# Attention in steps of two sequences, and a written order for TensorE in the middle blocks, in a fused retention, gated MLP and soft-MoE kernel

## The chip, the cores and the metric

One Trainium2 chip, one core. The metric is the device time of the whole kernel in microseconds (us). TensorE is called PE here, its weight loads PEld; VectorE is DVE, ScalarE ACT, GpSimd POOL, SyncE SP. SP's queue and ACT's queue issue the DMAs.

## What is computed

Three stages in a row, in float32, on 8 sequences of 576 tokens with 8 heads of 64 (4608 tokens, model width 512):

```python
scores = q @ k.T / sqrt(64);  ret = scores * gamma[h] ** (i - j)   # lower triangle only
x = heads_side_by_side(ret @ v)                                    # 4608 x 512
h = x @ w_in;  g = h * sigmoid(1.702 * h);  x = g @ w_out          # 512 -> 2048 -> 512
logits = x @ phi                                                   # 32 slots
d = softmax(logits, over tokens);  slot_input = d.T @ x            # 32 x 512
slot_out = 8 experts, 4 slots each: relu(slot_input @ w1) @ w2     # 512 -> 1024 -> 512
out = softmax(logits, over slots) @ slot_out                       # 4608 x 512
```

## The kernel before, in words

The 4608 tokens are cut into 12 blocks of 384 (`NB`), and a block's first MLP layer into 16 groups `fc` of 128 columns. `main_fc(n, fc)` (line 312) runs 12 matmuls into the PSUM tile `hp`: four 128-row pieces of x, each as high x high, high x low, low x high part (fp32r operands, full 128x128 weights, 384 columns). ACT writes the gated result to `gT`. `turn_fc` (324) turns each `gT` on DVE in 32x32 pieces, and after eight of them 16 DMAs on SP's queue finish the transposition into `nat` (line 349).

The second layer is never run over the tokens. w_out is folded with phi into `Wp` at the start, so `logits_group` (352) makes the expert scores `Lg` straight from `gT`, four matmuls a group on 32 weight columns each. `softmax_part(n)` (360) adds up the four parts with a matmul (`lt`), takes the running maximum, exponentiates to `dT`, and transposes it on PE (`dp`); `slots_part(n)` (400) accumulates `dn` times `nat` into `Sg`.

Attention makes x for the block after the one that the MLP is in. It goes in chunks of 64 tokens of one sequence, four head pairs. `chunk_out` (210) computes `Op`, eight matmuls of 128x64 weights; DVE scales it to `xs`, ACT rounds that to the high part of x and POOL subtracts to get the low part. `products` (175) adds the chunk's keys times values to the state `St` and multiplies keys and queries of the next chunk to `Sp`, both with 64x64 weights; DVE writes `St` and `Sp`, scaled by decay tables, back into the chunk's `pack` (lines 202, 203, 207, 208), from where the next `chunk_out` reads them. A chunk's q, k and v arrive by two DMAs of 256 KB, one on SP's queue and one on ACT's (`load_chunk`, 164); four packs rotate.

PE executes four weight shapes: 128x128 (`hp`, `lt`, and PE transposes of full size such as `tpw` and `tpg`), 128x64 (`Op`), 64x64 (`St`, `Sp`) and 128x32 (`Lg`, `Sg`); `dp` has a fifth, 64x128. A list `START` (50) orders the work of block 0, where the weights are loaded and split too. From block 1 on, the loop at line 489 emits the calls, chunks after the `fc` numbers in `CHUNK_AT` (55), and a scheduler with its own model of time puts the instructions of each engine in order. Block 11 has no attention beside it. In block 10 and after it the expert weights are prefetched (`prefetch`, 430), then come the experts and the output.

Of the kernel before, what the change touches and what calls it, by code (L numbers as in the profile page):

```python
# [38 lines left out]
NW2 = 9  # L39
# [15 lines left out]
CHUNK_AT = (0, 2, 5, 8, 10, 12)  # L55

# [55 lines left out]
def tile_kernel(ctx, tc, qkv, w_in, w_out, phi, w1, w2, consts, out):  # L112
# [44 lines left out]
    packs = []  # L157
    for i in range(NPACK):
        packs.append(pa.tile([128, 6, NP, C], F32, name=f"pack{i}", bufs=1))
    kts = [pa.tile([128, NP, D], F32, name=f"kt{i}", bufs=1) for i in range(2)]  # L160
# [3 lines left out]
    def load_chunk(g):  # L164
        t = packs[g % NPACK].rearrange("p c a d -> p (c a d)")
# [7 lines left out]
    halves = (slice(0, C), slice(C, 128))  # L173

    def products(g):

        n = g + 1
        more = g >= 0 and g % NPB < NPB - 1
        if more:
            if g % NPB == 0:  # L180
                St[g // NPB] = ps.tile([128, NP, D], F32, tag="St", name="St")
            s_, kk, t = St[g // NPB], kts[g % 2], packs[g % NPACK]
        if n < NT // C:
            u = packs[n % NPACK]
# [24 lines left out]

    def chunk_out(g):  # L210
        n, off = divmod(g * C, NB)
        t = packs[g % NPACK]
        Op = ps.tile([128, NP, C], F32, tag="r", name="Op", bufs=3)
        for p in range(NP):
            pe.matmul(Op[0:C, p, :], t[:, V0, p], t[:, Q0, p], start=True, stop=True)  # L215
            pe.matmul(Op[C:128, p, :], t[:, V1, p], t[:, Q1, p], start=True, stop=True)  # L216
# [3 lines left out]
        cols_ = slice(off, off + C)  # L220
        xs = pa.tile([128, NP, C], F32, tag="xs", name="xs")
        dve.tensor_tensor(xs, Op, osc, op=ALU.mult)  # L222
        act.copy(xh[n][:, :, cols_], xs)  # L223
        pool.tensor_tensor(xl[n][:, :, cols_], xs, xh[n][:, :, cols_], op=ALU.subtract)  # L224

    def chunk(g):

        if g + NPACK - 1 < NT // C:
            load_chunk(g + NPACK - 1)
        chunk_out(g)  # L230
        products(g)

    def chunk_items(n):

        if n >= NBLK:
            return []
        return [(CHUNK_AT[i], lambda g=g: chunk(g)) for i, g in enumerate(range(n * NB // C, (n + 1) * NB // C))]

# [70 lines left out]
    gT, pre, nat, Lg, dn = {}, {}, {}, {}, {}  # L309
    st = {"m": None, "corr": None}  # L310

    def main_fc(n, fc):
        g, fl = divmod(fc, GF)
        if fl == 0:
            gT[n, g] = pg.tile([128, GF, NB], F32, tag="gT", name="gT", bufs=2)
        hp = ps.tile([128, NB], F32, tag="h", name="hp", bufs=3)
        i = 0
        for dc in range(NDC):
            for a, b in ((0, xh), (0, xl), (1, xh)):
                pe.matmul(hp, wt[fc][:, a, dc, :], b[n][:, dc, :], start=(i == 0), stop=(i == 3 * NDC - 1))  # L320
                i += 1
        act.activation(gT[n, g][:, fl, :], hp, AF.Gelu_apprx_sigmoid)  # L322

    def turn_fc(n, fc):
# [19 lines left out]
        if fh == HF - 1:  # L344
            if hf == 0:
                nat[n] = pm.tile([128, NT128, 4, NFC, 32], F32, tag="nat", name="nat")
            for a in range(4):
                for b in range(4):
                    sp.dma_start(nat[n][32 * b:32 * b + 32, :, a, hf * HF:(hf + 1) * HF, :],
                                 pre[n, hf][32 * a:32 * a + 32, b])  # L350
# [8 lines left out]
    def softmax_part(n):  # L359
        Lp = pm.tile([128, 2, NB], F32R, tag="Lp", name="Lp")  # L360
# [28 lines left out]
        dp = ps.tile([128, NT128, 2 * NS], F32, tag="L", name="dp")  # L389
        for c in range(NT128):  # L390
            pe.transpose(dp[:, c, :], dT[0:2 * NS, c * 128:(c + 1) * 128], ident[0:2 * NS, 0:2 * NS])  # L391
# [5 lines left out]
                          mx.unsqueeze(2).to_broadcast([128, NT128, NS]), op=ALU.subtract)  # L397

# [25 lines left out]
    todo = [(0, i) for i in range(NFC // 2)] + first[9:] + second[:5] + first[:9] + second[5:]  # L424
# [31 lines left out]
    items = [lambda: products(-1)] + [lambda g=g: chunk(g) for g in range(2 * NB // C)]  # L456

    def step(x):
# [9 lines left out]
        elif x[0] == "A":  # L468
            items.pop(0)()
        elif x == "M":  # L470
            fc = st.setdefault("fc", 0)
            st["fc"] += 1
            main_fc(0, fc)
            turn_fc(0, fc)
            if fc % 4 == 1 and fc >= 5:
                logits_group(0, (fc - 5) // 4)
        elif x[0] == "T":
            load_chunk(int(x[1:]))
        else:
            raise ValueError(x)  # L480
# [6 lines left out]
    pw2 = None  # L487

    for n in range(1, NBLK):
        items = chunk_items(n + 1)  # L490
        ni, done = len(items), 0
        for fc in range(NFC):
            main_fc(n, fc)
            if n < LAST:
                turn_fc(n, fc)
            if fc == SOFTMAX_AT:
                softmax_part(n - 1)
                if n == LAST:
                    combine_part(0, NTILE - NT128)
            if fc == SLOTS_AT:  # L500
                slots_part(n - 1)
            while done < ni and items[done][0] <= fc:
                items[done][1]()
                done += 1
            if fc == 0:
                logits_group(n - 1, 3)
            if fc in LOGITS_AT:
                logits_group(n, LOGITS_AT[fc])
            if n == LAST - 1:
                if fc == 9:  # L510
                    prefetch_views(pb.tile([128, 3, 1024], F32, tag="pre", name="wx", bufs=1))
                if done == ni and pw2 is None:
                    att_ctx.close()
                    prefetch(place_in(px, "raw", 1))
                    pw2 = ctx.enter_context(tc.tile_pool(name="pw2", bufs=NW2, side="right", reuse_waits="tile"))
                    for _ in range(NW2):
                        prefetch(place_in(pw2, "w", NW2))
            if n == LAST:
                if fc == 0:
                    prefetch_views(pb.tile([128, 3, 1024], F32, tag="x", name="wx", bufs=1))  # L520
                prefetch(place_in(pw, "w", NFC))
                if fc == 4:
                    prefetch_views(ring.rearrange("p a b f -> p a (b f)"))
                for i in range(SLOTS_AT + 1 if fc == SLOTS_AT else fc > SLOTS_AT):
                    turn_fc(n, fc - (SLOTS_AT - i if fc == SLOTS_AT else 0))
# [203 lines left out]
```

## Time and profile before

| | |
|---|---|
| median of three runs | 757.02 us (756.02 to 758.18) |
| the profiled execution | 760.1 us |
| its span, first to last instruction | 758.3 us |
| mean granted PE clock over the span | 0.969 |
| PE busy, instructions | 709.8 us (94%), 7512 |
| PEld, DVE, ACT, POOL busy | 575.5, 378.2, 235.8, 117.3 us |

The page names each group of instructions by its line, its engine and its tiles (out<-in). In the timeline, equal neighbours stand in one row with their number; an fp32 matmul stands as two instructions, a transpose or an fp32r one as one. A row's length goes to its last end, and PE's instructions overlap, so how long a stretch of work holds PE is read from its start to the start of what follows.

### The profile page before, as it was taken

What the parts mean: (1) busy time and instruction counts of PE and PEld (TensorE: products, weight loads), DVE (VectorE), ACT (ScalarE), POOL (GpSimd) and SP (SyncE); (2) the same over time, 40 slices, a digit from 0 to 9 for tenths busy, and PEclk for the clock granted to TensorE, in tenths of its full rate; (3) what the DMA queues carried; (4) which work ended last, traced back from release to release, by engine and by line L of the source; (5) the groups of instructions that cost most, each with busy time, mean ns of one, the idle gap of its engine ahead of it and who ended that gap; (6) DMA issues with size and microseconds to landing.
All of it is one profiled execution on the core that took longest, in us unless ns stands there. A gap on an engine that the chain in (4) does not pass through costs nothing.

```text
span 758.3 us, 18421 instructions
## 1 busy us (share of the span) xinstructions
PE 709.8 (94%) x7512; PEld 575.5 (76%) x7512; DVE 378.2 (50%) x1136; ACT 235.8 (31%) x467; POOL 117.3 (15%) x169
## 2 busy tenths in 40 slices
PE   4549999999999999999999999999999999978995
PEld 3438787789798888887888878878889788752573
DVE  3757964545546445454455554645555542221233
ACT  1335642323124123241232232412322325231332
POOL 2323320111111111111111111112112010000000
PEclk9659999999999999999999999999999999998999
DMA  9998996475366654753566547635575279988987
GB/s 225 293 264 292 305 260 143 110 165 117 88 134 141 136 126 103 167 129 89 130 129 147 128 93 164 140 90 125 123 161 128 62 220 324 348 330 327 408 330 311
DMA packets 78292, 142.22 MB, mean 188 GB/s; under 512 B 10752, under 2 KB 52992, under 8 KB 78208
## 3 DMA queue, kind: packets, MB, share of 16 engines
q1 hardware_dynamic: 70144, 117.97, 56.2%
q10 hardware_dynamic: 8064, 23.07, 12.0%
q8 instruction: 59, 0.97, 0.6%
q14 instruction: 25, 0.20, 0.1%
HBM read 92.77 MB, written 13.63 MB: 140 GB/s over the span
## 4 chain that ended last, share of the span: by engine, by line
PE 87%; DVE 2%; ACT 1%; issue 0%; DVEq 0%; ACTq 0%
PE hp L320 54%; PE Lg L356 6%; PE Sg L404 5%; PE Op L215 4%; PE St L189 4%; PE so_ps L643 2%; PE Sp L193 2%; PE h_ps L579 2%; PE op L665 1%; PE Op L216 1%; PE lt L366 1%; PE tpg L332 1%; PE cp L615 1%; PE tpw L294 1%; PE dp L391 1%; PE si_ps L553 0%
## 5 line engine op out<-in xcount | busy, mean ns | idle before, releaser
L320 PE MATMUL hp<-x,w 128*128 128x384 f32 x2304 | 431.8, 342 | 11.3 <-ACT x L223 10.3
L320 PEld LDWEIGHTS hp<-x,w 128*128 128x128 f32 x2304 | 396.8, 189 | 43.3 <-issue 27.5
L322 ACT ACTIVATE gT<-hp 128x384 f32<-128x384 f32 x192 | 93.0, 491 | 268.4 <-PE hp L320 267.7
L343 DVE STREAM_TRANSPOSE ring<-gT 128x128 f32<-128x128 f32 x240 | 55.9, 284 | 113.3 <-ACT gT L322 113.3
L343 DVE STREAM_TRANSPOSE pre<-gT 128x128 f32<-128x128 f32 x288 | 64.4, 279 | 73.8 <-ACT gT L322 73.7
L198 POOL TENSOR_TENSOR kt<-pack,cs 128x256 f32<-128x256 f32 x64 | 42.4, 662 | 314.3 <-PE Sp L193 178.1
L224 POOL TENSOR_TENSOR x<-xs,x 128x256 fp32r<-128x256 f32 x72 | 54.2, 753 | 150.9 <-ACT x L223 148.4
L223 ACT CAST x<-xs 128x256 fp32r<-128x256 f32 x72 | 29.2, 405 | 136.5 <-DVE xs L222 100.4
L215 PEld LDWEIGHTS Op<-pack 128*64 128x64 f32 x576 | 42.0, 142 | 31.9 <-issue 24.1
L215 PE MATMUL Op<-pack 128*64 128x64 f32 x576 | 54.5, 235 | 9.0 <-DVE pack L207 9.0
L193 PE MATMUL Sp<-pack 64*64 64x64 f32 x1152 | 51.9, 232 | 7.5 <-DMA pack<-in_qkv_dram 7.5
L356 PE MATMUL Lg<-gT,Wp 128*32 128x384 f32 x384 | 52.4, 498 | 0.6 <-DVE Wp L304 0.6
L189 PE MATMUL St<-pack,kt 64*64 64x64 f32 x1024 | 49.2, 233 | 4.0 <-DVE pack L203 4.0
L216 PE MATMUL Op<-pack 128*64 128x64 f32 x576 | 51.0, 234 | 0.1
L189 PEld LDWEIGHTS St<-pack,kt 64*64 64x64 f32 x1024 | 38.9, 142 | 15.3 <-issue 11.2
L193 PEld LDWEIGHTS Sp<-pack 64*64 64x64 f32 x1152 | 41.6, 141 | 9.8 <-DMA pack<-in_qkv_dram 7.2
L216 PEld LDWEIGHTS Op<-pack 128*64 128x64 f32 x576 | 40.7, 142 | 4.0 <-issue 3.1
L404 PE MATMUL Sg<-nat,dn 128*32 128x512 f32 x288 | 38.0, 635 | 0.3 <-DVE dn L393 0.3
L207 DVE TENSOR_TENSOR pack<-Sp,cs 64x256 f32<-64x256 f32 x72 | 30.8, 428 | 8.8 <-DMA cs<-in_consts_dram 5.6
L202 DVE TENSOR_TENSOR pack<-St,cs 64x256 f32<-64x256 f32 x64 | 27.3, 426 | 12.5 <-PE St L189 10.8
L208 DVE TENSOR_TENSOR pack<-Sp,cs 64x256 f32<-64x256 f32 x72 | 30.0, 417 | 2.0
L222 DVE TENSOR_TENSOR xs<-Op,cs 128x256 f32<-128x256 f32 x72 | 28.6, 397 | 2.6 <-PE Op L216 2.5
(113 smaller groups left out, 479.3 us busy)
## 6 DMA issues: line engine op xcount, KB each, us to landing
wx<-in_moe_w_dram SPq DMA_DIRECT2D x56, 512.0 KB, 9.7
pack<-in_qkv_dram ACTq DMA_DIRECT2D x72, 256.0 KB, 4.6
pack<-in_qkv_dram SPq DMA_DIRECT2D x72, 256.0 KB, 4.6
nat<-pre SPq DMA_DIRECT2D x192, 96.0 KB, 3.0
nat<-ring SPq DMA_DIRECT2D x160, 96.0 KB, 3.1
out_dram<-ob SPq DMA_DIRECT2D x16, 512.0 KB, 3.8
early_raw<-in_moe_w_in_dram SPq DMA_DIRECT2D x14, 512.0 KB, 9.2
early_raw<-in_moe_w_out_dram SPq DMA_DIRECT2D x14, 512.0 KB, 7.0
```

The source lines that it names most:

```text
L189: pe.matmul(s_[h, p, :], kk[h, p, :], t[h, v, p], start=g % NPB == 0 and p == 0, stop=True, skip_group_check=True)
L193: pe.matmul(Sp[o, p, :], u[h, KT, p], u[h, q, p], start=True, stop=True)
L198: pool.tensor_tensor(kts[n % 2], u[:, KN], ksc[:, cb, :].unsqueeze(2).to_broadcast([128, NP, D]), op=ALU.mult)
L207: dve.tensor_tensor(u[C:128, Q0], Sp[C:128], dtab[C:128], op=ALU.mult)
L215: pe.matmul(Op[0:C, p, :], t[:, V0, p], t[:, Q0, p], start=True, stop=True)
L216: pe.matmul(Op[C:128, p, :], t[:, V1, p], t[:, Q1, p], start=True, stop=True)
L224: pool.tensor_tensor(xl[n][:, :, cols_], xs, xh[n][:, :, cols_], op=ALU.subtract)
L320: pe.matmul(hp, wt[fc][:, a, dc, :], b[n][:, dc, :], start=(i == 0), stop=(i == 3 * NDC - 1))
L322: act.activation(gT[n, g][:, fl, :], hp, AF.Gelu_apprx_sigmoid)
L343: dve.transpose(dst[:, c], src[:, c])
L356: pe.matmul(Lg[n][32 * fl:32 * fl + 32, :], Wp[:, g * GF + fl, :], gT[n, g][:, fl, :], start=(g == 0), stop=(g == NFC // GF - 1))
L404: pe.matmul(Sg[32 * b:32 * b + 32], dn[n][:, c, :], nv[:, 4 * b:4 * b + 4], start=(c == 0), stop=(c == NT128 - 1))
```

## The change

Attention now goes in 36 steps of 64 tokens of two sequences (`NSEQ`, `CP`), so three steps make a block of 384. The host lays q, k, v and the output out accordingly. A step has twice a chunk's matmuls, in the same shapes; the DVE, ACT and POOL instructions and the DMAs of a step have twice the elements. Three packs rotate instead of four, and the decayed keys are written in place (`KN`) instead of to `kts`.

In blocks 1 to 10 PE's instructions stay in the order in which the program writes them (`tc.manual_schedule`); the other engines' are still ordered by the scheduler. After `fc` 4, 9 and 13 (`WINDOWS`) stands a place: one step, then the groups of `Lg` that `WINDOW_LOGITS` names, and at the second place `Sg` too. `lt` stands after `fc` 5 and `dp` after `fc` 7; `softmax_part` is cut in three for that. `dp` transposes all 128 rows of `dT` with the full identity. The 16 DMAs into `nat` become a function of their own, `shuffle`, called at the second place and after `fc` 15. `gT` has three buffers instead of two. The descriptor memory asked for GpSimd's DMAs shrinks, and 11 instead of 9 expert weight tiles are prefetched into the space that attention leaves, `w2` tiles 6 and 7 ahead of nine of the first layer. Block 11 keeps its order of calls. `START` names six steps instead of twelve chunks.

```diff
-NW2 = 9
+NW2 = 11
-NPACK = 4
-PC = NP * C
+NPACK = 3
+NSEQ = 2
+CP = NSEQ * C
...
-    "T0 C T1 Id T2 P A A Id A I A A I A Id A M O I M A Id M O I M I A M O I M I A M O Id M I A M O I M Id A M O I "
+    "T0 C T1 Id P A A Id I A I A Id M O I M Id M O I M I A M O I M I M O Id M I A M O I M Id M O I "
-CHUNK_AT = (0, 2, 5, 8, 10, 12)
+WINDOWS = (4, 9, 13)
+WINDOW_LOGITS = ((1, 3),), ((0, 0), (0, 1)), ((0, 2),)
+SPLIT_AT, EXP_AT, TURN_AT = 4, 5, 7
...
         for p in range(NP):
-            if more:
-                for h, v in zip(halves, (V1, V0)):
-                    pe.matmul(s_[h, p, :], kk[h, p, :], t[h, v, p], start=g % NPB == 0 and p == 0, stop=True,
-                              skip_group_check=True)
+            for j in range(NSEQ):
+                if more:
+                    for h, v in zip(halves, (V1, V0)):
+                        pe.matmul(s_[h, p, j, :], t[h, KN, p, j], t[h, v, p, j], start=g % NPB + p + j == 0, stop=True,
+                                  skip_group_check=True)
...
-            gT[n, g] = pg.tile([128, GF, NB], F32, tag="gT", name="gT", bufs=2)
+            gT[n, g] = pg.tile([128, GF, NB], F32, tag="gT", name="gT", bufs=3)
...
-        dp = ps.tile([128, NT128, 2 * NS], F32, tag="L", name="dp")
+        dTs[n] = dT
+
+    def softmax_turn(n):
+        dT = dTs.pop(n)
+        dp = ps.tile([128, NT128, 128], F32, tag="L", name="dp")
         for c in range(NT128):
-            pe.transpose(dp[:, c, :], dT[0:2 * NS, c * 128:(c + 1) * 128], ident[0:2 * NS, 0:2 * NS])
+            pe.transpose(dp[:, c, :], dT[:, c * 128:(c + 1) * 128], ident)
...
-    todo = [(0, i) for i in range(NFC // 2)] + first[9:] + second[:5] + first[:9] + second[5:]
+    todo = [(0, i) for i in range(NFC // 2)] + first[9:] + second[:7] + first[:9] + second[7:]
...
+    with tc.manual_schedule(engines={mybir.EngineType.PE}):
+        for n in range(1, LAST):
+            for fc in range(NFC):
+                main_fc(n, fc)
                 turn_fc(n, fc)
+                if fc in WINDOWS:
+                    i = WINDOWS.index(fc)
+                    step_of((n + 1) * STEPS + i)
+                    for m, k in WINDOW_LOGITS[i]:
+                        logits_group(n - m, k)
+                    if i == 1:
+                        slots_part(n - 1)
+                        shuffle(n, 0)
+                if fc == SPLIT_AT:
+                    softmax_split(n - 1)
+                if fc == EXP_AT:
+                    softmax_exp(n - 1)
+                if fc == TURN_AT:
+                    softmax_turn(n - 1)
+                if fc == NFC - 1:
+                    shuffle(n, 1)
...
-    nc = _bacc.Bacc("TRN2", target_bir_lowering=False, num_devices=1)
+    nc = _bacc.Bacc("TRN2", target_bir_lowering=False, num_devices=1, dynamic_dma_scratch_size=1024)
```

PE before, in a middle block, around the transposes `dp` of the softmax (a row is a line, an instruction and its tiles, with the number of equal neighbours):

```order
L193 MATMUL Sp<-pack_95 64x64 x2
L320 MATMUL hp<-x,w 128x384 x31
L391 MATMUL dp<-ident,dT 128x64 x3
L320 MATMUL hp<-x,w 128x384 x5
L189 MATMUL St<-pack_95,kt_97 64x64 x8
L320 MATMUL hp<-x,w 128x384 x4
L404 MATMUL Sg<-nat,dn 32x512 x12
L215 MATMUL Op<-pack_95 64x64
```

The run of `hp` is cut by `dp`, by a chunk's `St` without its `Sp`, and by `Sg`. PE in the changed kernel, from the first place of a middle block towards the second (the step's 16 `Op` follow the last row):

```order
L198 MATMUL Sp<-pack_94 64x64 x2
L353 MATMUL Lg<-gT,Wp 32x384 x4
L316 MATMUL hp<-x,w 128x384 x12
L366 MATMUL lt<-Lp,sum4r 128x384 x2
L316 MATMUL hp<-x,w 128x384 x24
L395 MATMUL dp<-ident,dT 128x128 x3
L316 MATMUL hp<-x,w 128x384 x24
L221 MATMUL Op<-pack_94 64x64
```

Between two places only `lt` and `dp` now stand among the `hp`. Over blocks 1 to 10, PE's instructions leave a run of `hp` for another weight shape 79 times before and 31 times now, if the full-size transposes and `lt` are counted as `hp`'s own shape; neighbours of different shape are 299 before and 120 now.

DVE in the changed kernel at the first place of that block:

```order
L228 TENSOR_TENSOR xs<-Op,cs 128x512
L207 TENSOR_TENSOR pack_94<-St,cs 64x512
L208 TENSOR_TENSOR pack_94<-St,cs 64x512
L212 TENSOR_TENSOR pack_94<-Sp,cs 64x512
L213 TENSOR_TENSOR pack_94<-Sp,cs 64x512
L360 TENSOR_TENSOR Lp<-Lg,Lp 128x384
L339 STREAM_TRANSPOSE pre<-gT 128x4x32 x3
L368 TENSOR_REDUCE mb<-lt 128x1
```

`Lp`, the low part of the scores that `lt` multiplies, stands behind the step's four evictions; before, it stood behind a chunk's, with half the elements.

## Rows read from the trace of the kernel before

**Rows 1.** Page: PE's busy tenths and granted clock in 40 slices of the span.
```profile
PE   4549999999999999999999999999999999978995
PEclk9659999999999999999999999999999999998999
```
**Rows 2.** Busy us (x instructions) of PE, PEld, DVE, ACT, POOL; PEclk, DMA share, GB/s.
```profile
50.00:100.00 50.00, 45.72 (x540) 39.50 (x540) 43.19 (x94) 29.91 (x56) 19.24 (x17) 0.91 0.97 296
```
**Rows 3.** Timeline of PE: start, length, instruction; two runs of hp with what follows.
```profile
318.56 8.60 PE L320 MATMUL hp<-x,w 128*128 128x384 f32 x48
327.09 0.27 PE L215 MATMUL Op<-pack 128*64 128x64 f32 x1
...
329.11 4.43 PE L320 MATMUL hp<-x,w 128*128 128x384 f32 x24
333.47 0.33 PE L215 MATMUL Op<-pack 128*64 128x64 f32 x2
```
**Rows 4.** Timeline of PE: one chunk's Op, St and Sp, and Lg after them.
```profile
303.79 0.27 PE L215 MATMUL Op<-pack 128*64 128x64 f32 x1
...
304.13 0.22 PE L215 MATMUL Op<-pack 128*64 128x64 f32 x1
...
304.19 0.22 PE L215 MATMUL Op<-pack 128*64 128x64 f32 x1
...
304.41 0.27 PE L189 MATMUL St<-pack,kt 64*64 64x64 f32 x2
...
304.63 0.22 PE L189 MATMUL St<-pack,kt 64*64 64x64 f32 x2
...
304.69 0.23 PE L189 MATMUL St<-pack,kt 64*64 64x64 f32 x2
...
305.03 0.85 PE L356 MATMUL Lg<-gT,Wp 128*32 128x384 f32 x8
```
**Rows 5.** Timeline of PE: a lone pair of Lg, then lt inside Op, then dp.
```profile
315.79 0.83 PE L356 MATMUL Lg<-gT,Wp 128*32 128x384 f32 x2
316.55 0.27 PE L215 MATMUL Op<-pack 128*64 128x64 f32 x1
...
333.73 0.61 PE L366 MATMUL lt<-Lp,sum4r 128*128 128x384 f32 x2
334.27 0.27 PE L216 MATMUL Op<-pack 128*64 128x64 f32 x1
...
341.08 0.40 PE L391 MATMUL dp<-ident,dT 64*128 64x64 f32 x3
```
**Rows 6.** Timeline of PE in block 11: lt and full-size transposes among hp.
```profile
634.52 0.51 PE L366 MATMUL lt<-Lp,sum4r 128*128 128x384 f32 x2
634.87 6.07 PE L320 MATMUL hp<-x,w 128*128 128x384 f32 x34
...
659.60 0.49 PE L332 MATMUL tpg<-ident,gT 128*128 128x128 f32 x3
659.84 0.77 PE L320 MATMUL hp<-x,w 128*128 128x384 f32 x3
```
**Rows 7.** Timeline of DVE: a chunk's evictions, from the first to Lp.
```profile
328.81 0.43 DVE L202 TENSOR_TENSOR pack<-St,cs 64x256 f32<-64x256 f32 x1
...
330.16 0.42 DVE L208 TENSOR_TENSOR pack<-Sp,cs 64x256 f32<-64x256 f32 x1
330.50 0.54 DVE L363 TENSOR_TENSOR Lp<-Lg,Lp 128x384 fp32r<-128x384 f32 x1
```
**Rows 8.** Groups by line: DVE copies of 512 PSUM elements (busy us, mean ns).
```profile
L666 DVE COPY ob<-op 128x512 f32<-128x512 f32 x18 | 11.7, 687 | 9.4 <-PE op L665 9.4
```
**Rows 9.** Chain that ended last, behind block 11: the last lt and dp.
```profile
677.41 0.64 PE lt L366 x2
...
680.35 0.59 PE dp L391 x3
```
**Rows 10.** Waits of PE: us in total, times, longest.
```profile
PE hp L320 <- ACT x L223: 10.3, 1, 10.3
```

More of the change, by code (lines that the diff above doesn't have):

```diff
@@ L156, in tile_kernel, with load_step @@
     early_raw = pm.tile([128, 6, 1024], F32, tag="nat", name="early_raw")
[L157 to L160, printed above, removed]
+    packs = [pa.tile([128, 6, NP, NSEQ, C], F32, name=f"pack{i}", bufs=1) for i in range(NPACK)]
     pool.memset(packs[0][0:C, V0], 0.0)
     pool.memset(packs[0][C:128, V1], 0.0)
-    def load_chunk(g):
-        t = packs[g % NPACK].rearrange("p c a d -> p (c a d)")
+    def load_step(g):
+        t = packs[g % NPACK].rearrange("p c a j d -> p (c a j d)")
         sp.dma_start(t[0:C, KT * PC:6 * PC], qkv[g, 0:C])
@@ L219, in chunk_out, with step_of @@
             xh[n], xl[n] = x[:, 0], x[:, 1]
[L220 to L230, printed above, removed]
+        cols_ = slice(i * CP, (i + 1) * CP)
+        xs = pa.tile([128, NP, NSEQ, C], F32, tag="xs", name="xs")
+        dve.tensor_tensor(xs, Op, osc.unsqueeze(2).to_broadcast([128, NP, NSEQ, C]), op=ALU.mult)
+        flat = xs.rearrange("p a j c -> p a (j c)")
+        act.copy(xh[n][:, :, cols_], flat)
+        pool.tensor_tensor(xl[n][:, :, cols_], flat, xh[n][:, :, cols_], op=ALU.subtract)
+    def step_of(g):
+        if g + NPACK - 1 < NSTEP:
+            load_step(g + NPACK - 1)
+        step_out(g)
         products(g)
[L233 to L237, printed above, removed]
     wt = {}
@@ L343, in turn_fc, with shuffle @@
             dve.transpose(dst[:, c], src[:, c])
[L344 to L350, printed above, removed]
+    def shuffle(n, hf):
+        if hf == 0:
+            nat[n] = pm.tile([128, NT128, 4, NFC, 32], F32, tag="nat", name="nat")
+        for a in range(4):
+            for b in range(4):
+                sp.dma_start(nat[n][32 * b:32 * b + 32, :, a, hf * HF:(hf + 1) * HF, :],
+                             pre[n, hf][32 * a:32 * a + 32, b])
     def logits_group(n, g):
@@ L357, in logits_group, with softmax_split @@
                       start=(g == 0), stop=(g == NFC // GF - 1))
[L359 to L360 removed]
+    def softmax_split(n):
+        Lp = Lps[n] = pm.tile([128, 2, NB], F32R, tag="Lp", name="Lp")
         lg = Lg.pop(n)
@@ L455, in tile_kernel @@
     outs = [lambda i=i: make_wp(i) for i in range(NFC // 2)]
-    items = [lambda: products(-1)] + [lambda g=g: chunk(g) for g in range(2 * NB // C)]
+    items = [lambda: products(-1)] + [lambda g=g: step_of(g) for g in range(2 * STEPS)]
     def step(x):
@@ L474, in step @@
             turn_fc(0, fc)
+            if fc % HF == HF - 1:
+                shuffle(0, fc // HF)
             if fc % 4 == 1 and fc >= 5:
@@ L486, in tile_kernel @@
         step(x)
[L487 to L494, printed above, removed]
-                turn_fc(n, fc)
[L496 to L525, printed above, removed]
@@ new lines, in tile_kernel @@
+    with tc.manual_schedule(engines={mybir.EngineType.PE}):
+        for n in range(1, LAST):
+            for fc in range(NFC):
+                main_fc(n, fc)
+                turn_fc(n, fc)
+                if fc in WINDOWS:
[14 more added lines that the diff above has]
+                    shuffle(n, 1)
+                if n == LAST - 1:
+                    if fc == 11:
+                        prefetch_views(pb.tile([128, 3, 1024], F32, tag="pre", name="wx", bufs=1))
+                    if fc == WINDOWS[-1]:
+                        att_ctx.close()
+                        prefetch(place_in(px, "raw", 1))
+                        pw2 = ctx.enter_context(tc.tile_pool(name="pw2", bufs=NW2, side="right", reuse_waits="tile"))
+                        for _ in range(NW2):
+                            prefetch(place_in(pw2, "w", NW2))
@@ new lines, in tile_kernel @@
+    n = LAST
+    for fc in range(NFC):
+        main_fc(n, fc)
+        if fc == SOFTMAX_AT:
+            softmax_part(n - 1)
+            combine_part(0, NTILE - NT128)
+        if fc == SLOTS_AT:
+            slots_part(n - 1)
+        if fc == 0:
+            logits_group(n - 1, 3)
+        if fc in LOGITS_AT:
+            logits_group(n, LOGITS_AT[fc])
+        if fc == 0:
+            prefetch_views(pb.tile([128, 3, 1024], F32, tag="x", name="wx", bufs=1))
+        prefetch(place_in(pw, "w", NFC))
+        if fc == 4:
+            prefetch_views(ring.rearrange("p a b f -> p a (b f)"))
+        for i in range(SLOTS_AT + 1 if fc == SLOTS_AT else fc > SLOTS_AT):
+            turn_fc(n, fc - (SLOTS_AT - i if fc == SLOTS_AT else 0))
```

71 lines of the change are left out of this document (43 added, 28 removed).

## Prediction, made before the changed kernel was run

> **What bounds the kernel now.** I read the page's slices first. PE is full from slice 4 to slice 35 of 40, and its granted clock is 9 tenths or more there [rows 1], the 2.4 GHz level, with no cold stretch. At the start it is not PE: from 50 to 100 us PE is busy 45.7 of 50 us, while the DMA engines are at 0.97 and DVE works 43.2 us [rows 2], and before its first `hp` PE waited 10.3 us for x [rows 10]. So in blocks 1 to 10 only what PE itself spends counts, and a wait of PE counts in full.
>
> PE being "busy" there is not PE at its best, so next I took from the timeline what a run of equal work holds, from its start to the start of what follows. A run of 48 `hp` holds 327.09 - 318.56 = 8.53 us, one of 24 holds 333.47 - 329.11 = 4.36 [rows 3]. The 24 more cost 4.17, so an `hp` costs 0.174 and each run has 0.18 us that belongs to no matmul. The same with a chunk: its `Op` holds 304.41 - 303.79 = 0.62 us; inside the run a pair of instructions comes every 0.06, eight pairs make 0.48, and 0.14 is fixed. `St` and `Sp` together hold 305.03 - 304.41 = 0.62 with the same step of 0.06 for four instructions, so 0.14 is fixed there as well [rows 4]. The fixed parts lie where one weight shape follows another. They are what this change can touch: the matmuls stay the same in number and shape, but for `dp`.
>
> **The change part by part, blocks 1 to 10 (30 steps for 60 chunks).** The counts are counted along the order of the two programs.
>
> - Runs of `hp`: 79 before, 31 now, if `lt` and the full-size transposes do not end a run. That they do not is seen in block 11: two `lt` among `hp` hold 634.87 - 634.52 = 0.35, as two `hp` would, and three transposes hold 0.24 [rows 6]. 48 x 0.18 = 8.6 us less.
> - `Op`: one run a step in place of two, 30 x 0.14 = 4.2 less. `St` with `Sp`: the same, 4.2 less.
> - `St` standing apart: the scheduler had set it as a run of its own 7 times, which holds 8 x 0.06 + 0.14 = 0.62 and then costs nothing extra inside the joint run: 4.3. Six times a single `St` was cut off: 6 x 0.14 = 0.8.
> - `lt`: before it cut into an `Op` run and held 334.27 - 333.73 = 0.54 [rows 5]; now 0.35 as above. 10 x 0.19 + 9 cuts x 0.14 = 3.2 less.
> - `Lg`: in four places a pair stood alone, and a lone pair held 316.55 - 315.79 = 0.76 [rows 5]. Now the groups of four stay whole: 3.0 less. Behind `Lg` there now comes `Lg` or `Sg`, of its own shape, 20 times; half of the 0.18 of an `hp` run, 0.09, for each: 1.8.
> - `dp` goes from 64 to 128 columns of identity; three transposes for three, taken at nothing.
>
> Sum: 8.6 + 4.2 + 4.2 + 5.1 + 3.2 + 4.8 = 30 us less on PE.
>
> What the written order may cost is a wait. **`lt` now stands 12 `hp` behind the first place**, and needs `Lp`, which DVE makes behind the step's four evictions. Count from the step's first `Op`: its run holds 16 x 0.06 + 0.14 = 1.10, `St` and `Sp` another 1.10, `Lg` about 0.76, the `hp` 12 x 0.174 + 0.09: PE is ready for `lt` at 5.1. DVE can begin the evictions when the last `Sp` has ended, at 2.2 + 0.2. An eviction of 64x256 took 0.43 and came every 0.45 [rows 7]. None of 64x512 is in the trace: below it is not under 0.43, above not over 0.86. I take 0.69, because a DVE copy of 512 elements out of PSUM took 0.687 [rows 8]. Four at 0.71 and `Lp` at 0.54 [rows 7] end at 5.8: PE waits 0.65 us in each block, 6.5 in all. With the bounds of the eviction it is 0 to 13. What queues behind it is all of PE, so this comes off the gain in full.
>
> **`dp` stands 24 `hp` behind `lt`**, 0.35 + 4.18 = 4.5 us after it. Between them lie the maximum, the exponential and a copy. Bare, at the end of the program, this took 680.35 - 677.41 = 2.9 us from `lt` to `dp` [rows 9]; in a middle block they stood 341.08 - 333.73 = 7.35 apart, as the scheduler put them [rows 5]. I take no wait; the bounds are 0 and 2.8 a block.
>
> Edits taken at nothing in the middle, with their cover: twice the elements for DVE, ACT and POOL in each step (they have idle time, and fewer instructions in all); the same bytes in half as many loads, with three packs: a pack is refilled once its step is over and needed two places on, at the least nine `fc` or 9 x 12 x 0.174 = 19 us later, and 1 MB at the 296 GB/s of a full stretch [rows 2] is 3.5 us. SP's half of a load can stand behind the 16 DMAs of `shuffle`; the same distance covers it. If that cover went, `Sp` at a place would wait. `gT` with three buffers makes room for the later `Lg`; no engine works longer for it.
>
> Start and end I take at nothing. At the start the bytes are the same; DVE saves the fixed parts of 30 evictions, the first load is twice as long. In block 11 and behind it PE's work is the same, and the prefetch begins at about the same distance from the block's end. Each is uncertain by 5 us both ways.
>
> Net: 30 - 6.5 = 23.5 us less. Against the profiled execution, 760.1 us with a span of 758.3, this gives 736.6; it ran 3.1 us over the median of the runs, 757.0. Against that median: **733.5 us**.
>
> **The rivals.** *A change of shape gives back less.* The fixed 0.18 of an `hp` run has two changes in it, 0.09 each; if that is all a change costs anywhere, and the rest of the fixed parts belongs to the work and stays, then the fall from 299 to 120 neighbours of different shape brings 179 x 0.09 = 16, less 6.5 of wait: 747.4 us. For it: 0.18 is the price that I measured on the longest runs. Against it: `Op` and `St` show 0.14 for each run besides, and the lone pairs are real work that goes. The Trainium skill has a rule of this kind: "TensorEngine Tiling (Array Packing)", Key Properties, says that changing the tiling mode, and not merely the tile, drains the engine; "TensorE: Matmul & The Clock Gate", Part 2, puts a drain at about 128 cycles. By these pages a change would cost 53 ns at 2.4 GHz, an estimate, 179 of them 9.5 us, and the kernel would come to 754. The rows agree that it is the shape that costs (`lt` and full transposes cost nothing extra) and put the price higher. Chance 0.13.
>
> *No wait at `lt`.* The evictions are quicker, or DVE begins them earlier: all 30 us come, 727 us. Chance 0.12.
>
> *The softmax becomes the bound: slower.* If `lt` to `dp` needs all of the 7.35 us that it had, because ACT and DVE are at other work, `dp` waits 2.8 us in each block beside the 0.65 at `lt`: 34.5 against 30, or 761.5 us. It decides from 2.35 us of wait at `dp`. For it: the order is fixed, so PE can no longer do other work meanwhile. Against it: the bare chain of 2.9 us leaves 1.6 of room. Chance 0.04.
>
> *Nothing comes of it*, the freed time being lost again at the ends: within a few us of 757, chance 0.05.
>
> **How the numbers follow.** 0.66 for the forecast, with its own range of 727 to 741 from the ends' 5 us and half of the wait's bounds. The range of 723 to 748 takes in the second rival with a better start and the first; left out are the slower rival, the standstill and the tails of the others, under 0.2. What a measurement can tell from no change is about 0.3%, 2.3 us. Faster by more: 0.66 + 0.13 + 0.12 and part of the standstill, 0.93; within it 0.03; slower 0.04.
>
> **What would show it.** After, `hp` runs of 84 (with `lt` and `dp` inside) and of 48 should hold no more than 0.18 each beyond their matmuls; a step's `Op` should hold 1.10; a block should come about 2.4 us sooner after the one before it; PE's only new wait should be `lt` on `Lp`, some 0.6 us, ten times, and DVE's 64x512 evictions should take about 0.69. It is wrong if `dp`, `Sp` or `Sg` waits in each block, if the `Op` of a step holds 1.24, or if the time before block 1 or behind block 10 grows by over 5 us.

## The result and the profile after

The changed kernel took 737.96 us (median of four runs, 735.42 to 739.44) against 757.38 us (756.02 to 758.18) for the kernel before beside it: 0.9742 of its time, 95% interval 0.9711 to 0.9773. The forecast was 733.5 with a range of 723 to 748. Its profiled execution has a span of 736.5 us against 758.3, at a mean granted clock of 0.970 against 0.969.

The page of the changed kernel: PE's busy time and instructions, then the 40 slices of PE and its clock that answer to [rows 1], then one of DVE's evictions (busy us, mean ns).

```profile
PE 675.6 (92%) x7512; PEld 567.7 (77%) x7512; DVE 349.5 (47%) x964; ACT 230.9 (31%) x431; POOL 103.1 (14%) x93
...
PE   2549999699999999999999999999999999978995
...
PEclk9769999989999999999999999999999999999999
...
L212 DVE TENSOR_TENSOR pack<-Sp,cs 64x512 f32<-64x512 f32 x36 | 25.0, 694 | 11.0 <-PE Sp L198 10.2
```

PE executes the same number of instructions and is busy 34 us less. A 64x512 eviction takes 0.694 us, the 0.69 of the forecast. Behind the start, one thing is new in the slices: the eighth, some 129 to 147 us, has PE at 6 tenths, and the one behind it has the clock at 8.

**A middle block.** The timeline of PE from the first place of block 3 (start, length, instruction; in brackets the idle time before it and what ended it):

```profile
234.06 0.27 PE L221 MATMUL Op<-pack 128*64 128x64 f32 x1
...
235.14 0.27 PE L194 MATMUL St<-pack 64*64 64x64 f32 x2
...
236.23 0.85 PE L353 MATMUL Lg<-gT,Wp 128*32 128x384 f32 x8
237.01 2.35 PE L316 MATMUL hp<-x,w 128*128 128x384 f32 x12
239.67 0.61 PE L366 MATMUL lt<-Lp,sum4r 128*128 128x384 f32 x2 [0.31 <-DVE Lp L360]
240.12 4.34 PE L316 MATMUL hp<-x,w 128*128 128x384 f32 x24
244.30 0.49 PE L395 MATMUL dp<-ident,dT 128*128 128x128 f32 x3
244.54 4.41 PE L316 MATMUL hp<-x,w 128*128 128x384 f32 x24
```

`Op` holds 235.14 - 234.06 = 1.08 us, `St` and `Sp` 1.09, where a chunk's had held 0.62 each [rows 4]; twice that would be 1.24. In this block `lt` is the only instruction that waits. What it waits for stands in the timeline of DVE for the same place:

```profile
236.36 0.69 DVE L207 TENSOR_TENSOR pack<-St,cs 64x512 f32<-64x512 f32 x1 [0.34 <-PE Sp L198]
...
238.47 0.68 DVE L213 TENSOR_TENSOR pack<-Sp,cs 64x512 f32<-64x512 f32 x1
239.08 0.54 DVE L360 TENSOR_TENSOR Lp<-Lg,Lp 128x384 fp32r<-128x384 f32 x1
```

`Lp` ends at 239.62, 5.56 us after the first `Op`; the forecast had 5.8.

**Where the time went.** Of a middle block the instruction that adds `Sg` to `acc` can serve as a clock; it stands once a block. In the timeline of DVE, blocks 2 and 10 of the kernel before:

```profile
196.60 0.75 DVE L410 SCALAR_TENSOR_TENSOR acc<-acc,corr,Sg 128x512 f32<-128x512 f32 x1 [2.16 <-PE Sg L404]
...
596.65 0.75 DVE L410 SCALAR_TENSOR_TENSOR acc<-acc,corr,Sg 128x512 f32<-128x512 f32 x1 [2.15 <-PE Sg L404]
```

and of the changed kernel:

```profile
207.93 0.75 DVE L419 SCALAR_TENSOR_TENSOR acc<-acc,corr,Sg 128x512 f32<-128x512 f32 x1 [1.18 <-PE Sg L413]
...
587.04 0.75 DVE L419 SCALAR_TENSOR_TENSOR acc<-acc,corr,Sg 128x512 f32<-128x512 f32 x1 [1.21 <-PE Sg L413]
```

A block lasts (596.65 - 196.60) / 8 = 50.01 us before and (587.04 - 207.93) / 8 = 47.39 after. I use this "length of a block" for every kernel below. The ends of the program can be split off by counting `hp` (192 a block) in the two traces: block 1 begins at 121.88 and now at 119.07, block 2 at 174.65 and 176.09, block 11 at 624.77 and 601.57. So the span's 21.8 us are made of 2.8 less before block 1, **4.2 more in block 1**, 24.6 less in blocks 2 to 10, and 1.4 more from block 11 on.

From block 1 on, two waits of PE grew (us in total, times, longest); the kernel before had 2.3 us of `dp` and 1.2 of `lt`, once each and both behind block 11:

```profile
PE dp L395 <- DVE dT L386: 9.8, 2, 6.1
...
PE lt L366 <- DVE Lp L360: 3.4, 11, 0.4
```

At the start the waits changed both ways: that for x fell from 10.3 us [rows 10] to 7.0, that of `Sp` for the first load, which is now twice as large, rose from 7.2 to 13.5. The first `hp` comes 1.4 us later than before, and block 0 is 4.2 us shorter (65.0 against 69.2); that makes the 2.8.

**Block 1.** The 6.1 us of `dp` are there; its other 3.7 stand behind block 11. The timeline of PE around them:

```profile
146.87 0.87 PE L395 MATMUL dp<-ident,dT 128*128 128x128 f32 x3 [6.10 <-DVE dT L386]
147.39 6.86 PE L316 MATMUL hp<-x,w 128*128 128x384 f32 x24
154.18 0.27 PE L221 MATMUL Op<-pack 128*64 128x64 f32 x1
```

and for the same time SP's issues into `nat` and the timeline of DVE:

```profile
126.50 11.81 SPq L346 DMA_DIRECT2D nat<-pre  x16
...
136.63 0.56 DVE L368 TENSOR_REDUCE mb<-lt 128x1 f32<-128x384 f32 x1 [0.70 <-PE lt L366]
141.31 3.59 DVE L339 STREAM_TRANSPOSE pre<-gT 128x128 f32<-128x128 f32 x18 [4.12 <-DMA nat<-pre]
144.83 0.11 DVE L375 TENSOR_SCALAR negm<-mb 128x1 f32<-128x1 f32 x1
...
146.17 0.55 DVE L386 COPY dT<-lt 32x384 f32<-32x384 f32 x1
```

The maximum `mb` is ready at 137.2, but the negative `negm` that the exponential needs comes at 144.8. Ahead of it DVE has 18 transposes into `pre`, and the first stood 4.12 us until the DMAs that read `pre` for block 0 were done: block 0 puts both its halves through the one buffer `pre`, and SP issues the 16 transfers of the second from 126.5 to 138.3. In the rows `negm` runs only behind those 18, so a softmax that needs nothing of `pre` waits with it. The kernel before met the same 16 transfers. Its DVE, in the same stretch:

```profile
133.07 0.56 DVE L368 TENSOR_REDUCE mb<-lt 128x1 f32<-128x384 f32 x1 [0.42 <-PE lt L366]
...
134.44 0.13 DVE L375 TENSOR_SCALAR negm<-mb 128x1 f32<-128x1 f32 x1
...
135.48 0.55 DVE L386 COPY dT<-lt 32x384 f32<-32x384 f32 x1
...
140.72 3.60 DVE L343 STREAM_TRANSPOSE pre<-gT 128x128 f32<-128x128 f32 x18
```

There the softmax's operations stood ahead of the 18 transposes, which ran without a wait. The wait costs more than its 6.1 us: the 24 `hp` behind it hold 154.18 - 147.39 = 6.79 us, where 24 hold 4.36 [rows 3]. The stretches of 141 to 154 us of the changed kernel (busy us of PE, PEld, DVE, ACT and POOL with their instructions; granted clock, DMA share, GB/s) say why:

```profile
141.00:147.00 6.00, 0.14 (x1) 0.17 (x2) 5.40 (x27) 2.25 (x4) 1.04 (x1) 0.91 0.25 57
147.00:150.00 3.00, 3.00 (x11) 3.00 (x12) 0.68 (x3) 0.00 (x0) 0.00 (x0) 0.50 0.03 5
150.00:152.00 2.00, 2.00 (x7) 2.00 (x7) 0.00 (x0) 0.34 (x1) 0.00 (x0) 0.50 0.00 0
152.00:154.00 2.00, 2.00 (x11) 1.93 (x10) 0.52 (x3) 1.44 (x2) 0.00 (x0) 0.83 0.00 0
```

PE came back at a granted clock of 0.50, the 1.2 GHz level, and was at full clock again only after 152. Wait and clock together are 6.1 + 2.4 = 8.5 us, of 57.02 - 47.39 = 9.6 by which block 1 is longer than a middle block.

### The profile page after: what moved, and what is told of

Same layout as the page of the kernel before. It is cut to its first block, busy times and chain, and to the rows that moved or that the text cites. A ratio compares the mean times of both kernels' runs of the same rounds, so it can differ in the third digit from the quotient of the medians.

```text
span 736.5 us, 17854 instructions
## 1 busy us (share of the span) xinstructions
PE 675.6 (92%) x7512; PEld 567.7 (77%) x7512; DVE 349.5 (47%) x964; ACT 230.9 (31%) x431; POOL 103.1 (14%) x93
## 4 chain that ended last, share of the span: by engine, by line
PE 77%; DMA 9%; DVE 7%; SPq 4%; issue 1%; ACT 1%; DVEq 0%; ACTq 0%
PE hp L316 49%; DMA early_raw<-in_moe_w_in_dram 6%; PE Sg L413 5%; PE Op L221 4%; PE Lg L353 4%; PE St L194 3%; PE h_ps L600 3%; PE so_ps L664 3%; SPq L346 2%; DMA pack<-in_qkv_dram 2%; DMA nat<-pre 2%; PE Sp L198 1%; DVE pre L339 1%; SPq L255 1%; PE op L686 1%
## 5 line engine op out<-in xcount | busy, mean ns | idle before, releaser
L231 POOL TENSOR_TENSOR x<-xs,x 128x512 fp32r<-128x512 f32 x36 | 46.6, 1296 | 242.7 <-ACT x L230 236.8
L203 POOL TENSOR_TENSOR pack<-pack,cs 128x512 f32<-128x512 f32 x32 | 34.4, 1075 | 179.0 <-DMA pack<-in_qkv_dram 151.7
L198 PE MATMUL Sp<-pack 64*64 64x64 f32 x1152 | 44.2, 228 | 13.5 <-DMA pack<-in_qkv_dram 13.5
L198 PEld LDWEIGHTS Sp<-pack 64*64 64x64 f32 x1152 | 38.6, 140 | 14.5 <-DMA pack<-in_qkv_dram 13.5
L194 PE MATMUL St<-pack 64*64 64x64 f32 x1024 | 40.6, 230 | 9.3 <-DVE pack L208 8.9
L221 PE MATMUL Op<-pack 128*64 128x64 f32 x576 | 44.0, 231 | 4.4 <-DVE pack L212 4.4
L194 PEld LDWEIGHTS St<-pack 64*64 64x64 f32 x1024 | 35.4, 142 | 14.6 <-issue 12.3
L222 PE MATMUL Op<-pack 128*64 128x64 f32 x576 | 43.0, 231 | 0.0
L230 ACT CAST x<-xs 128x512 fp32r<-128x512 f32 x36 | 22.2, 618 | 52.3 <-DVE xs L228 43.8
L212 DVE TENSOR_TENSOR pack<-Sp,cs 64x512 f32<-64x512 f32 x36 | 25.0, 694 | 11.0 <-PE Sp L198 10.2
L228 DVE TENSOR_TENSOR xs<-Op,cs 128x512 f32<-128x512 f32 x36 | 24.5, 682 | 5.4 <-PE Op L222 5.4
L207 DVE TENSOR_TENSOR pack<-St,cs 64x512 f32<-64x512 f32 x32 | 22.2, 693 | 8.6 <-PE Sp L198 8.4
L413 PEld LDWEIGHTS Sg<-nat,dn 128*32 128x32 f32 x288 | 9.5, 113 | 20.5 <-issue 19.7
```

The costliest lines, as they stand in the source:

```text
L194: pe.matmul(s_[h, p, j, :], t[h, KN, p, j], t[h, v, p, j], start=g % NPB + p + j == 0, stop=True, skip_group_check=True)
L198: pe.matmul(Sp[o, p, j, :], u[h, KT, p, j], u[h, q, p, j], start=True, stop=True)
L203: pool.tensor_tensor(u[:, KN], u[:, KN], by_state(ksc[:, cb, :], 128), op=ALU.mult)
L212: dve.tensor_tensor(u[hi, Q0], Sp[hi], by_head(dtab, hi), op=ALU.mult)
L221: pe.matmul(Op[0:C, p, j, :], t[:, V0, p, j], t[:, Q0, p, j], start=True, stop=True)
L222: pe.matmul(Op[C:128, p, j, :], t[:, V1, p, j], t[:, Q1, p, j], start=True, stop=True)
```

## The experiments

Every kernel was timed beside the kernel before on the same chip; ratios are to that. The changed kernel's is 0.974, its block 47.39 us.

**1. One sequence a chunk, but in the written order.** Chunks of 64 tokens of one sequence as before, at six places a block, with `START` as in the kernel before; `Lg`, `Sg`, `lt` and `dp` stand at the same `fc` as in the changed kernel.

```diff
-NPACK = 3
-NSEQ = 2
+NPACK = 4
+NSEQ = 1
...
-WINDOWS = (4, 9, 13)
-WINDOW_LOGITS = ((1, 3),), ((0, 0), (0, 1)), ((0, 2),)
+WINDOWS = (2, 4, 7, 9, 11, 13)
+WINDOW_LOGITS = (), ((1, 3),), (), ((0, 0), (0, 1)), (), ((0, 2),)
```

> The changed kernel with chunks of one sequence again (NSEQ = 1, four packs, the start order of the kernel before) in TensorE's written order, with six places a block for them in place of three; the Lg, Sg, lt and dp stand at the same fc as in the changed kernel. Theory (what a run of one shape holds beside its matmuls is what the change saved): 30 more hp runs in blocks 1 to 10 at 0.18, 30 more Op runs and 30 more St/Sp runs at 0.14 each, 13.8 us; less at most 3 us if the wait of lt goes; about 3 us more at the start, as there before: 749 to 755 us, a block of 2 to 10 at 48.6 to 48.8 us against 47.4 now and 50.0 before. Rival (it is the written order that brings the gain, not the fewer and wider steps): 736 to 741 us, blocks of 47.4. Rival (0.09 for each change of shape, 90 changes more): 8.1 us and the start, 746 to 749.

Measured: 740.34 us against 759.67, 0.9754 (0.971 to 0.9797), block 48.27 us.

```profile
202.81 0.75 DVE L419 SCALAR_TENSOR_TENSOR acc<-acc,corr,Sg 128x512 f32<-128x512 f32 x1 [1.95 <-PE Sg L413]
...
588.96 0.75 DVE L419 SCALAR_TENSOR_TENSOR acc<-acc,corr,Sg 128x512 f32<-128x512 f32 x1 [1.95 <-PE Sg L413]
```

By the time alone this looks like the rival, that the written order is everything, and my 749 to 755 us was missed; so were my blocks of 48.6 to 48.8. The blocks decide against the rival, which had them at 47.4. The order, with the wide `dp` in it, brings 50.01 - 48.27 = 1.74 us a block. The wide steps bring another 0.88, and that is net of a wait: here `lt` does not wait, since a chunk's evictions are shorter (0.43 us against 0.69, [rows 7]). The time comes out equal because this kernel loses less in block 1 (52.2 us against 57.0; `dp` waits 3.2 us there) and its profile is 2.4 us shorter from block 11 on. I had taken off nothing for either, and put 3 us more at the start, where it has 0.7 less.

**2. Wide steps, but the scheduler's order.** The line `with tc.manual_schedule(...)` taken away.

> The changed kernel without the written order: the steps of two sequences and the three places stand in the program as now, but TensorE's order in the middle blocks is the scheduler's. By the built program it puts lt into a run of Op in 9 to 11 blocks, and dp elsewhere, with 33 hp runs in place of 31. Theory (wide steps and few places do it, the written order hardly anything): lt inside Op costs 0.33 a block (0.19 of its own and 0.14 for the second Op run), 3.3 us, and the wait of lt on Lp goes or stays within 3 us: 735 to 741 us. Rival (the written order carries a large part of the gain): over 745 us.

Measured: 731.28 us, 0.963 (0.960 to 0.966), **faster than the changed kernel**, and below my 735 to 741. A block is 47.21 us, from `acc` at 204.30 and 581.94. From its timeline of PE in block 5:

```profile
328.04 5.82 PE L316 MATMUL hp<-x,w 128*128 128x384 f32 x32
333.70 0.51 PE L366 MATMUL lt<-Lp,sum4r 128*128 128x384 f32 x2
334.04 5.03 PE L316 MATMUL hp<-x,w 128*128 128x384 f32 x28
339.00 0.27 PE L221 MATMUL Op<-pack 128*64 128x64 f32 x1
...
339.39 0.55 PE L395 MATMUL dp<-ident,dT 128*128 128x128 f32 x3
...
340.71 0.27 PE L194 MATMUL St<-pack 64*64 64x64 f32 x2
```

I had put `lt` into `Op`; it is `dp` that stands there. The two together hold 340.71 - 339.00 = 1.71, where apart they hold 1.08 + 0.24: 0.39 more. `lt` has 32 `hp` ahead of it and does not wait. In block 1 `dp` waits 0.5 us, and the block lasts 49.1 us; block 0 is 4.1 longer than the changed kernel's (69.1 against 65.0). So the few long runs come from the program, which calls the work at three places, and the scheduler keeps them; holding PE to the exact order brought the wait at `lt` and most of the loss in block 1.

**3. `Op` at a place of its own.**

```diff
...
+                if fc + 1 in WINDOWS:
+                    out_of((n + 1) * STEPS + WINDOWS.index(fc + 1))
                 if fc in WINDOWS:
                     i = WINDOWS.index(fc)
-                    step_of((n + 1) * STEPS + i)
+                    products((n + 1) * STEPS + i)
```

(`out_of` is the first half of `step_of`: the load and `Op`.)

> The changed kernel with Op put one fc ahead of the rest of its step, so that every step has two places: in blocks 1 to 10 there are 30 more hp runs and 30 more changes of shape, and nothing else is added. Theory (0.18 us for every hp run): 5.4 us more, 742 to 745 us, and the time from the last hp ahead of Op to the first Op plus the time lost behind Op adds up to 0.18 at each of the 30. Rival (0.09 for each change of shape): 2.7 us more, 739.5 to 742. Rival (a change costs nothing, the fixed parts were the filling of the work itself): 737 to 739.

Measured: 743.0 us, 0.9784 (0.9753 to 0.9814), block 48.14 us (`acc` at 209.51 and 594.65), 0.75 more. The run of 12 `hp` between `Op` and `St`, in its timeline of PE:

```profile
233.73 0.27 PE L221 MATMUL Op<-pack 128*64 128x64 f32 x1
...
234.81 2.35 PE L319 MATMUL hp<-x,w 128*128 128x384 f32 x12
237.10 0.27 PE L194 MATMUL St<-pack 64*64 64x64 f32 x2
...
241.81 0.62 PE L369 MATMUL lt<-Lp,sum4r 128*128 128x384 f32 x2 [0.47 <-DVE Lp L363]
```

The 12 `hp` hold 2.29 us, 0.20 more than 12 x 0.174. `Op` still holds 234.81 - 233.73 = 1.08, so nothing is taken from it when `St` no longer follows. Three such runs are 0.61 a block, and `lt` waits 0.16 longer; that is the 0.75. (By the medians the kernel lost 5.0 us and by the ratios 3, instead of 7.5; its profile is 2.5 us shorter from block 11 on. The blocks decide.) The price of a run is 0.18 to 0.20, and the rival with 0.09 for the one further change of shape falls. From start to start the 0.20 has two parts: the last `hp` before another shape lasts 0.268 instead of 0.173, the first after it 0.28.

**4. `lt` one `fc` later.**

```diff
-SPLIT_AT, EXP_AT, TURN_AT = 4, 5, 7
+SPLIT_AT, EXP_AT, TURN_AT = 4, 6, 8
```

> The changed kernel with lt one fc later (EXP_AT 6 in place of 5, TURN_AT 8 in place of 7): 24 hp between the first place and lt, 24 between lt and dp as now. Theory: lt waits no more (3.4 us over all now, 0.31 a block), dp has as much room as now: 3 us less, 733.5 to 736 us, no PE wait of lt above 0.05 in blocks 2 to 10. Rival (the wait moves to dp or Sg, which now come 2.1 us later and nearer the second place): 737 to 740 us, with new waits of dp or Sg of 0.3 a block.

Measured: 730.3 us, 0.9621 (0.9584 to 0.9658), block 46.82 us (`acc` at 205.36 and 579.95).

```profile
234.46 4.43 PE L316 MATMUL hp<-x,w 128*128 128x384 f32 x24
238.72 0.51 PE L366 MATMUL lt<-Lp,sum4r 128*128 128x384 f32 x2
239.07 4.34 PE L316 MATMUL hp<-x,w 128*128 128x384 f32 x24
243.25 0.49 PE L395 MATMUL dp<-ident,dT 128*128 128x128 f32 x3
```

The wait is gone and did not move. A block gains 0.57 us, though the list of waits had shown only 0.31 for each `lt`. From start to start the sum is right: 12 `hp` behind `Lg` end their issue 2.19 us after 237.01 (0.28 + 11 x 0.174), so `lt` was due at 239.20 and came at 239.67, 0.47 late; and `lt` itself held 240.12 - 239.67 = 0.45 instead of 0.35. Together 0.57. Idle time in the profile begins at the modelled end of the matmul before, which lies later than its issue. The Trainium skill ("Perfetto Trace Analysis", Tensor Engine Instruction) says the same of the ends: the profiler computes them from the size of the instruction, it does not see them. By the ratios this kernel gains 1.2%, 9 us, where I had expected 3 and ten blocks give 5.7. Of the rest 1.1 us lie in block 1 (55.4 against 57.0) and 2.5 from block 11 on (124.6 us to PE's last matmul against 127.1). The latter I take for scatter, since from there on PE's order is the same in both programs; the mean granted clock of that stretch is 0.96 in the changed kernel and 0.97 here, which would make about half of the 2.5.

**5. The two buffers exchanged.** Behind block 0, half 0 of a block goes into the ring, half 1 into `pre`; the two prefetches that fill these buffers at the end are exchanged with them.

```diff
-            if n > 0 and hf:
+            if n > 0 and not hf:
                 pre[n, hf] = ring_pre
...
```

> The changed kernel with the two buffers for the halves of the transposed gates exchanged behind block 0: half 0 goes into the ring and half 1 into pre (and the prefetch takes them in the exchanged order). Block 1 then doesn't write first into the buffer that the 16 transfers of block 0 still read. Theory (block 1's loss is DVE standing at a transpose into pre, with the softmax's small operations queued behind it, and the clock at 1.2 GHz for 5 us after the wait): dp's wait of 6.1 us in block 1 goes, and so do the 2.5 us by which the 24 hp behind it were longer: block 1 at 48 to 49 us in place of 57.0, the whole 8 to 9 us less, 0.960 to 0.965 of the kernel before. Rival (the wait moves to where half 1 is written, or to Sg for the late transfers): block 1 at 54 to 57, 0.97 to 0.975.

Measured: 727.94 us against 760.65, 0.9572 (0.9547 to 0.9598), a little below my 0.960 to 0.965. A middle block stays at 47.39 (`acc` at 199.18 and 578.29), block 1 falls from 57.02 to 48.04 us. In block 1, the timeline of DVE and then that of PE:

```profile
137.01 0.52 DVE L368 TENSOR_REDUCE mb<-lt 128x1 f32<-128x384 f32 x1
137.57 0.15 DVE L375 TENSOR_SCALAR negm<-mb 128x1 f32<-128x1 f32 x1
```

```profile
140.77 0.49 PE L395 MATMUL dp<-ident,dT 128*128 128x128 f32 x3
141.01 4.41 PE L316 MATMUL hp<-x,w 128*128 128x384 f32 x24
```

`negm` follows the maximum at once, `dp` does not wait, and the 24 `hp` behind it are back at their usual length. Both the 6.1 us and the 2.4 us of slow clock went; the wait came back nowhere behind block 0. The spans differ by 10.7 us: 9.0 in block 1 and 1.9 from block 11 on (125.2 us to PE's last matmul against 127.1), less than one and the same order scattered there (experiment 4).

**6. `dp` narrow again.**

```diff
-        dp = ps.tile([128, NT128, 128], F32, tag="L", name="dp")
+        dp = ps.tile([128, NT128, 2 * NS], F32, tag="L", name="dp")
...
-            pe.transpose(dp[:, c, :], dT[:, c * 128:(c + 1) * 128], ident)
+            pe.transpose(dp[:, c, :], dT[0:2 * NS, c * 128:(c + 1) * 128], ident[0:2 * NS, 0:2 * NS])
```

> The changed kernel with dp as before, three transposes with 64 rows of dT and 64 columns of ident in place of the full size; that adds 20 changes of shape in blocks 1 to 10. Theory (a change of shape costs about 0.1 us on each side, the transposes themselves little): the stretch from the last hp ahead of dp to the second hp behind it grows by 0.18 to 0.28 us, a block by the same, 1.8 to 2.8 us over all: 0.976 to 0.979 of the kernel before, too near to the changed kernel's 0.974 to tell by the time alone, so the blocks of 2 to 10 decide: 47.55 to 47.65 us in place of 47.37. Rival (the size of the transposes decides, half the columns are half the work): blocks the same or up to 0.1 shorter.

Measured: 740.03 us, 0.9741 (0.9702 to 0.9781), and a block of 47.60 us (`acc` at 207.85 and 588.61), 0.21 more.

```profile
240.06 4.33 PE L316 MATMUL hp<-x,w 128*128 128x384 f32 x24
244.32 0.40 PE L395 MATMUL dp<-ident,dT 64*128 64x64 f32 x3
244.65 4.46 PE L316 MATMUL hp<-x,w 128*128 128x384 f32 x24
```

The run ahead holds 4.26 us against 4.18 with the full transposes, and `dp` 0.33 against 0.24, though it moves half the columns. The rest, some 0.04, is in the first `hp` behind. As expected, the whole time cannot tell 2 us; the blocks can. The wide `dp` is worth 2.1 us over ten blocks. The forecast had 1.8 of that without saying so: ten of its 48 runs of `hp` were those that the narrow `dp` had cut. What it took at nothing, the transposes themselves, are the 0.09 a block.

**7. Both mends together** (4 and 5).

> Both mends in one: the exchanged buffers, and lt one fc later (EXP_AT 6, TURN_AT 8). Theory (the two losses are separate): 0.9621 for the later lt, less 8.5 us for block 1: 0.950 to 0.953 of the kernel before, 720 to 724 us, block 1 at 47 to 48.5 us and blocks 2 to 10 at 46.85. Rival (the losses share a cause, or the exchange costs at the end, where the weights are fetched in another order): 0.957 to 0.962, or a tail longer by more than 3 us.

Measured: **723.21 us (722.38 to 724.68) against 760.65, 0.9517 (0.9491 to 0.9542)**: faster than both kernels. Block 1 lasts 47.47 us, a middle block 46.82 (`acc` at 198.00 and 572.59). The losses are separate. The profiled execution does have 128.0 us from block 11 to PE's last matmul, 3.4 more than in experiment 4, which was the rival's sign. But experiment 5, with the same exchange, had 125.2, and experiment 6 without it 128.0, so the exchange does not do it alone. The scheduler, which orders PE from block 11 on, sets the `cp` matmuls among those of the experts otherwise in each of these kernels (experiment 4 alone has the changed kernel's order); whether that or scatter makes the 3 us stays open.

**8. Both mends, but the scheduler's order.**

> The same two mends without the written order of TensorE: the scheduler keeps 33 hp runs against 31 and puts dp inside an Op run in most blocks. Theory (the written order is worth only the few runs that it saves): dp inside Op costs 0.5 us a block (one more Op run at 0.14, two changes of shape at about 0.1 each and one more entry of the transposes), at most: 0 to 5 us slower than the written order with both mends, 0.950 to 0.960. Rival (the written order still holds PE at waits that the scheduler avoids): faster than with the written order by 1 us or more, 0.945 to 0.950.

Measured: 730.64 us, 0.961 (0.9585 to 0.9635), 7.4 us slower than with the written order, where I had expected 5 at most. A block is 47.21 us, the 47.21 of experiment 2, against 46.82: 3.9 us over ten, the size of what `dp` in `Op` costs there (0.39). Block 2 begins at 172.3 us against 166.7; 2.3 of these 5.6 are there before the first `hp` (56.4 against 54.1). Block 0 takes 3.8 more (68.9 against 65.1), block 1 0.5 less. The scheduler orders block 0 in both kernels, but here it cuts `St` and `Sp` out of their steps at more places. Over all ten kernels block 0 lasts 64.5 to 65.5 us where the blocks behind it have the written order, and 68.9 to 69.2 where they have not (the kernel before, experiments 2 and 8). Why stays open. So the written order is worth something once its two waits are gone, and the mends bring the scheduler's order nothing: it had neither wait.

## Why the prediction was right, point by point

- **Runs of `hp`, `Op`, `St` and `Sp`** (17 of the 30 us) were right. Experiment 1 against experiment 4, neither with a wait at `lt`, is the measure of twice as many places: 48.27 - 46.82 = 1.45 us a block, where 3 x (0.18 + 0.14 + 0.14) = 1.38 was the price.
- **The terms of the order** (the other runs of `hp`, those that `dp` cut among them, `St` apart, `lt` and `Lg`) come to 18 x 0.18 + 5.1 + 3.2 + 4.8 = 16.3 us; experiment 1 against the kernel before shows 1.74 a block, 17.4.
- **`lt` on `Lp`** was right in place and nearly in size: 0.65 a block forecast, 0.57 measured by its removal. The list of waits alone, with 3.4 us, would have made the forecast look twice too high.
- All of it: 2.35 us a block forecast, 50.01 - 47.39 = 2.62 measured. Of the 0.27 between, 0.08 is the wait, and nearly all of the rest a sum that was 0.17 too low. Added up from start to start over blocks 2 to 9, the kernel before against experiment 4 (the changed order without the wait): `Op` gave 0.70 a block for 0.55 forecast (an `Op` run cut by `lt` holds 0.25 more, not 0.14), `St` and `Sp` 1.03 for 0.93, `Lg` with `Sg` 0.46 for 0.48, `lt` 0.20 for 0.19, `dp` 0.08 for nothing, but the runs of `hp` only 0.71 for 0.86.
- **The signs.** A step's `Op` held 1.08 us where 1.10 was named, and the evictions took the 0.69. Two signs were off. The run of `hp` with `lt` and `dp` inside is 60 long, not 84; the one of 84 has neither. And where no run was to hold over 0.18 beyond its matmuls, those of 48 held 8.54 us, 0.19 more, and those of 84 held 14.79 to 14.96, 0.17 to 0.34 more.
- **"`dp`: I take no wait"** is the step that failed, in one block of ten. The bound of 2.8 us a block was read from middle blocks. Block 1 was taken to be like them, but it writes first into a buffer that block 0's DMAs still read, and DVE carried that wait over to a softmax that had nothing to do with it. It cost 9.0 us (experiment 5). The row was there to be read: the kernel before has the same 18 transposes in one row. The slower rival named the right instruction with the wrong cause; it needed a wait in every block, and blocks 2 to 10 have none.
- **The ends**, taken at 0 with 5 us both ways: 2.8 less before block 1 and 1.4 more from block 11 on. The 2.8 are what is left of a block 0 that is 4.2 shorter, as under every written order (experiment 8), when the first `hp` comes 1.4 later. The changed kernel and experiment 4, with the same PE order from block 11 on, differ by 2.5 us there, so the second is within scatter.
- **The price of a change.** The rival's 0.09 falls with experiment 3. The Trainium skill says ("TensorEngine Tiling (Array Packing)", Key Properties) that a change of tiling mode drains the engine. The rows agree that a change costs: what stays in the shape (`lt`, the wide `dp`) costs nothing extra, what leaves it does; that it is a drain no run shows. The 53 ns that the prediction estimated from the Trainium skill ("TensorE: Matmul & The Clock Gate", Part 2) is about half of the 0.1 us measured on each side.

In sum: the forecast made 736.6 us of the profiled execution of before; that of the change, the first of the four runs, took 738.3. Block 1 is 6.6 us above the forecast (57.02 against 52.77 - 2.35), blocks 2 to 10 are 3.5 below (24.64 gained against 9 x 2.35), the start 2.8 below, the end 1.4 above: 1.7 together. That the total came so near is luck in part, since 8.0 us one way met 6.3 the other. The rest of the 4.5 us between 733.5 and 738.0 is the 3.1 by which before's profiled execution had run over its median; the change's did not.

## What to carry to other kernels

Price a change of order from start to start in the timeline: what a run holds beyond its matmuls, times the runs that go, gave the gain of a middle block here to about a tenth. When an order is written out, look at the first pass through the loop apart from the steady one, for each engine that the fixed one waits for: what is queued ahead of the operation that it needs, and what does *that* wait for. And measure the order by itself: here the few and wide places brought the gain of a middle block under either order (2.62 and 2.80 us), the written order with narrow chunks brought 1.74 of it, and the fixed order became worth its place only when its two waits had been moved out of its way.

## What the runs showed of the hardware

- A run of full-size fp32r matmuls that is cut by another weight shape costs 0.20 us: about 0.095 on the last one before and 0.107 on the first one behind. Three transposes with half the columns but another shape cost more (0.33 us and 0.12 around them) than three of the full size (0.24).
- An idle time of 0.31 us of PE, as the profile lists it, cost 0.57 us from start to start (experiment 4).
- After 6.1 us without work PE resumed at 0.50 of its clock, the 1.2 GHz level, and 24 `hp` held 6.79 us instead of 4.36: the wait cost 1.4 times its own length.
